# Sliding-window attention followed by a SiLU MLP: transposing q, k and the attention output by DMA over a DRAM scratch from the third batch on

## The chip, the cores and the metric

The kernel runs on one core of one Trainium2 chip. The metric is the device time of one execution in microseconds (us). The core has these engines: TensorE (PE; its weight loads are PEld), VectorE (DVE), ScalarE (ACT), GpSimd (POOL) and SyncE (SP). Besides them there are 16 DMA engines. In this kernel two of the engines issue DMAs: POOL, whose DMAs go through the software queue (q0), and SP, whose DMAs go through the hardware queue (q1).

Executions come in states: a run over 1.5% above the fastest of its kernel is called slow, and a single run has an unknown state.

## The reference, cut to what matters

```python
B, H, S, D = 8, 8, 576, 64          # batches, heads, tokens, head size
mask_plain = (rel >= 0) & (rel < 32)                        # heads 0..3
mask_dil   = (rel >= 0) & (rel < 128) & (rel % 4 == 0)      # heads 4..7
attn = softmax(where(mask, q @ k.T / 8, -1e9)) @ v
x = attn.transpose(0, 2, 1, 3).reshape(4608, 512)
h = x @ w_in                                                # 512 -> 2048
return (h * sigmoid(h)) @ w_out                             # 2048 -> 512
```

Inputs and outputs are float32. The kernel computes in float16. The MLP is by far the larger part of the arithmetic. Attention needs only a narrow band of scores, but in both kernels here it takes q and k with the head size on the partitions, and it hands its output to the MLP with the model size on the partitions. That is where the transposes come from.

## The kernel before

Each batch of attention loads q, k and v with converting DMAs from POOL (float32 in DRAM, float16 in SBUF). The token order is regrouped by `m, r` (token = 4m + r), so that a dilated head is a dense band in each residue r.

```python
def issue_qk(b):                       # four loads a batch, rows of 256 elements
    ...
        rows = src[b].rearrange("h (m r) d -> m h (r d)", r=DIL)
        for d, at in ((tiles[nm], m0), (rests[b % 2][p0 : p0 + MR], r0)):
            nc.gpsimd.dma_start(out=d.rearrange("p h r d -> p h (r d)"),
                                in_=rows[at : at + d.shape[0]])
def issue_v(b):                        # three loads a batch
    ...
    nc.gpsimd.dma_start(out=vp[:, j0:, :D], in_=win)      # rows of 64 elements
```

TensorE transposes q and k into PSUM, ACT and DVE evacuate them. After attention, TensorE transposes the output again, and a copy puts it in `xT`, in the regrouped token order:

```python
def trans_d(ring, h):
    for rp in range(2):
        for i, key in enumerate(("k", "rest", "q")):
            nc.tensor.transpose(tps[:, rp, i],
                loads[b][key][:, HN + h, 2 * rp : 2 * rp + 2, :], ident[:MA, :MA])
    yield "DVE", 0.40
    nc.vector.tensor_copy(...)
def x_d(ring, r):
    ...                                # 4 TensorE transposes
    dst = x_b[:, HP // 2 :, r * M : (r + 1) * M]          # contiguous
    ...                                # ACT copies it for batch 0, DVE for the others
    nc.vector.tensor_copy(dst, src)
```

The MLP works on groups of 512 tokens. A small planner in the Python code places attention steps between the four-matmul steps of the MLP and so fixes the order of the instructions on each engine. An output block leaves through `ob` (two buffers) with stores issued by SP.

The softmax here doesn't subtract the row's maximum and nothing guards it: scores larger than these inputs give would overflow.

## Time and profile before

| | before |
|---|---|
| median of 3 runs | 348.2 us (347.77 to 349.5) |
| PE busy | 325.1 us, 93% of the span |
| PE matmul instructions | 2656 |

The page of the profile comes first: the busy time of each engine, then rows with one digit for each of 40 equal slices of the span (9 is 90% busy or more), then the hardware DMA queue with packets, MB and the share of the 16 engines' time.

```profile
PE 325.1 (93%) x2656; PEld 165.1 (47%) x2656; DVE 221.7 (64%) x602; ACT 168.5 (48%) x322; POOL 53.1 (15%) x74
...
PE   0688898999989999999999999999999999999995
...
DMA  8999999929913972990589110100111200201232
...
q1 hardware_dynamic: 5632, 9.44, 9.1%
```

TensorE is the limit. DMA is full in the first 70 us or so (weights and the first batches of inputs), busy in bursts until about 190 us, and quiet after that. Next come the windows of 20 us. The columns are the busy time of PE, PEld, DVE, ACT and POOL (with instruction counts), the TensorE clock that the throttle granted as a share of full speed, the DMA share (1.00 is 16 engines' worth of packet time; overlapping packets count more than once) and GB/s.

```profile
120.00:140.00 20.00, 20.00 (x197) 10.71 (x198) 14.84 (x40) 11.21 (x23) 3.34 (x5) 1.00 0.59 69
200.00:220.00 20.00, 20.00 (x192) 10.02 (x190) 12.71 (x36) 11.95 (x25) 0.00 (x0) 1.00 0.10 28
```

From 120 us on TensorE is busy 20.00 of 20 us at full clock. Every microsecond of matmul taken away there should come off the time, unless it comes back as a wait.

This is one of the copies that put a transposed attention output in place. The view shows the engine, the duration in ns as minimum, median and maximum, when it ran, and the shape.

```profile
L421 DVE COPY xT<-xd_0_932 x1: 293/293/293, 65.0 to 65.0; 128x288 f16<-128x288 f16 x1
```

### The profile page before, as it was taken

The numbers are of one execution on the slowest core, as the hardware profiler recorded it, in microseconds if no ns is written. First come the engines' busy times: TensorE is split into PE (matmuls) and PEld (weight loads), VectorE is DVE, ScalarE is ACT, GpSimd is POOL, SyncE is SP. The second block draws the span as 40 slices with busy tenths as digits, with TensorE's granted clock in tenths as the row PEclk, the third lists the DMA queues.
The fourth block names the chain that finished last, engine by engine and source line by source line (L and its number), as shares of the span: only waits on it lengthen the run. The fifth ranks groups of instructions, "written<-read, shape, count | busy, mean of one in ns | idle before, by whom it ended". The sixth has DMA issues, their size and how long they took to land.

```text
span 348.7 us, 6693 instructions
## 1 busy us (share of the span) xinstructions
PE 325.1 (93%) x2656; PEld 165.1 (47%) x2656; DVE 221.7 (64%) x602; ACT 168.5 (48%) x322; POOL 53.1 (15%) x74
## 2 busy tenths in 40 slices
PE   0688898999989999999999999999999999999995
PEld 0553444555445455445554555455545444444442
DVE  4394777758888895888498739883986255054100
ACT  1453664076457546554644464546554254244211
POOL 8724344020203302030311000000000000000000
PEclk9999998999999999999999999999999999999999
DMA  8999999929913972990589110100111200201232
GB/s 107 188 205 199 200 181 169 189 53 141 109 30 37 178 55 59 132 120 32 89 127 103 31 36 27 32 32 30 32 31 32 60 11 22 77 14 32 61 82 70
DMA packets 59920, 29.80 MB, mean 85 GB/s; under 512 B 26608, under 2 KB 55280, under 8 KB 59888
## 3 DMA queue, kind: packets, MB, share of 16 engines
q0 software_dynamic: 54256, 19.92, 51.5%
q1 hardware_dynamic: 5632, 9.44, 9.1%
q8 instruction: 21, 0.34, 0.4%
q14 instruction: 11, 0.09, 0.1%
HBM read 39.84 MB, written 9.44 MB: 141 GB/s over the span
## 4 chain that ended last, share of the span: by engine, by line
PE 84%; DVE 9%; ACT 3%; DMA 2%; issue 1%; POOL 1%; ACTq 0%; POOLq 0%
DMA rest_111<-in_q_dram 2%; DVE gT_1066 L509 1%; PE y_1_892 L526 1%; PE y_3_3599 L526 1%; PE y_3_3089 L526 1%; PE y_3_2568 L526 1%; PE y_2_965 L526 1%; PE y_0_2117 L526 1%; PE y_0_664 L526 1%; PE y_3_4542 L526 1%; PE y_2_2464 L526 1%; PE y_2_2984 L526 1%; PE y_1_3338 L526 1%; PE y_1_3848 L526 1%; PE y_2_3495 L526 1%; PE y_3_1985 L526 1%
## 5 line engine op out<-in xcount | busy, mean ns | idle before, releaser
L498 PEld LDWEIGHTS <-w_in_83 128*128 128x128 f16 x576 | 52.8, 98 | 57.2 <-issue 6.1
L526 PEld LDWEIGHTS <-gT_4055 128*128 128x128 f16 x64 | 6.3, 98 | 7.5
L526 PEld LDWEIGHTS <-gT_3654 128*128 128x128 f16 x64 | 6.3, 98 | 7.6
L526 PEld LDWEIGHTS <-gT_4267 128*128 128x128 f16 x64 | 6.2, 97 | 7.6
L526 PEld LDWEIGHTS <-gT_3144 128*128 128x128 f16 x64 | 5.9, 98 | 6.4
L526 PEld LDWEIGHTS <-gT_519 128*128 128x128 f16 x64 | 5.8, 101 | 6.3 <-issue 1.4
L105 POOL DMA_DIRECT2D vraw_100<-in_v_dram x8 | 5.4, 678 | 20.7 <-DVE vd_98 L359 18.3
L105 POOL DMA_DIRECT2D vraw_101<-in_v_dram x8 | 5.4, 678 | 20.5 <-DVE vd_99 L359 14.7
L526 PEld LDWEIGHTS <-gT_1066 128*128 128x128 f16 x64 | 5.7, 98 | 5.8 <-DVE gT_1066 L509 0.4
L526 PEld LDWEIGHTS <-gT_2629 128*128 128x128 f16 x64 | 5.6, 97 | 5.1
L526 PEld LDWEIGHTS <-gT_2070 128*128 128x128 f16 x64 | 5.6, 97 | 5.1
L526 PEld LDWEIGHTS <-gT_1525 128*128 128x128 f16 x64 | 5.5, 97 | 4.9
L290 PE MATMUL td_0_205<-ident,k_nat_115 96*128 96x96 f16 x2 | 0.5, 272 | 6.6 <-DMA k_nat_115<-in_k_dram 6.6
L121 POOL DMA_DIRECT2D vp_97<-in_v_dram x4 | 5.7, 1432 | 1.5 <-DMA q_nat_167<-in_q_dram 1.4
L121 POOL DMA_DIRECT2D vp_96<-in_v_dram x4 | 5.8, 1444 | 0.6 <-PE td_3_678 L290 0.5
L290 PEld LDWEIGHTS <-rest_111 96*128 96x128 f16 x32 | 3.5, 108 | 5.1 <-issue 4.5
L311 PEld LDWEIGHTS <-kP_106 64*128 64x128 f16 x96 | 3.1, 100 | 5.7 <-issue 5.4
L273 ACT COPY kP_106<-ta_0_224 128x384 f16<-128x384 f16 x1 | 0.5, 479 | 10.9 <-PE ta_0_224 L270 10.9
L509 DVE SCALAR_TENSOR_TENSOR gT_4267<-th_0_4281,h_0_4268 128x512 f16<-128x512 f32 x1 | 0.7, 689 | 7.9 <-ACT th_0_4281 L507 7.9
L328 PEld LDWEIGHTS <-kqD_105 64*128 64x128 f16 x128 | 2.9, 97 | 5.8 <-issue 5.1
L365 PEld LDWEIGHTS <-probs_86 128*128 128x128 f16 x48 | 4.1, 100 | 3.1 <-DVE o_d_199 L368 0.8
L328 PEld LDWEIGHTS <-kqD_104 64*128 64x128 f16 x128 | 3.2, 102 | 5.2 <-issue 4.7
(1782 smaller groups left out, 1014.7 us busy)
## 6 DMA issues: line engine op xcount, KB each, us to landing
w_in_83<-in_moe_w_in_dram POOLq DMA_DIRECT2D x4, 512.0 KB, 12.1
w_out_84<-in_moe_w_out_dram POOLq DMA_DIRECT2D x4, 512.0 KB, 16.2
vp_97<-in_v_dram POOLq DMA_DIRECT2D x4, 384.0 KB, 10.8
vp_96<-in_v_dram POOLq DMA_DIRECT2D x3, 384.0 KB, 6.4
vraw_100<-in_v_dram POOLq DMA_DIRECT2D x4, 224.0 KB, 5.5
vraw_101<-in_v_dram POOLq DMA_DIRECT2D x4, 224.0 KB, 8.3
rest_111<-in_k_dram POOLq DMA_DIRECT2D x4, 192.0 KB, 6.2
rest_111<-in_q_dram POOLq DMA_DIRECT2D x4, 192.0 KB, 7.7
```

The lines of the kernel that those rows point to most:

```text
L105: nc.gpsimd.dma_start(out=vraw[p0 : p0 + m1 - m0, ab].rearrange("p h r d -> p h (r d)"), in_=src[m0:m1],)
L121: nc.gpsimd.dma_start(out=vp[:, j0:, :D], in_=win)
L273: nc.scalar.copy(kt[:, :MA], tps[:, 0].rearrange("p r m -> p m r"))
L290: nc.tensor.transpose(tps[:, rp, i], loads[b][key][:, HN + h, 2 * rp : 2 * rp + 2, :], ident[:MA, :MA],)
L311: nc.tensor.matmul(sp[i][:, QB * jj : QB * (jj + 1)], kP[r, hp, QB * j : QB * j + P], qP[r, hp, :, QM * j : QM * (j + 1)], start=True, sto ...
L328: nc.tensor.matmul(sp[i][:, c : c + MH], kqD[r, h, rp, 0, ab * KB : ab * KB + P], kqD[r, h, rp, 1, ab * MH : (ab + 1) * MH], start=True, s ...
L365: nc.tensor.matmul(a[:, i, : D + 1], lhs(i), rhs(i), start=True, stop=True)
L498: nc.tensor.matmul(h, w_in16[:, c, f * P : (f + 1) * P], xT[:, c, t0 : t0 + GT], start=(c == 0), stop=(c == HP - 1),)
L509: nc.vector.scalar_tensor_tensor(gTs[g][:, f], th, 1.0, h, ALU.add, ALU.mult)
L526: nc.tensor.matmul(y, gTs[g][:, f, tb * P : (tb + 1) * P], w_out16[:, f], start=(f == 0), stop=(f == NFF - 1),)
```

## The change

The intent is to take the transposes of q, k and the attention output off TensorE. Batches 0 and 1 keep the TensorE path. From batch 2 on, POOL issues a DMA that casts q and k into a float16 scratch in DRAM (a "cast"). SP then issues DMA transposes that read the scratch and write q and k transposed into SBUF (a "q/k turn": two instructions for heads 0 to 3 and two for heads 4 to 7). The attention output goes to another DRAM scratch, `x_s`, and comes back transposed, one group at a time (an "output turn"). Tokens keep their natural order, and the scores of a batch are made in 6 sets instead of 8.

```diff
-    xT = cpool.tile([P, HP, NT], F16, name="xT")
+    xA = cpool.tile([P, HP, GA * GT], F16, name="xA")                 # GA = 3
+    xRs = [cpool.tile([P, HP, GT], F16, name=f"xR_{i}") for i in range(XR)]  # XR = 3
+    kq_s = {b: dram.tile([2, H * S * D], F16, name=f"kq_s{b}") for b in range(PEB, B)}
+    x_s = dram.tile([NT, DM], F16, name="x_s")
...
+    def issue_cast(b):
+        for i, src in enumerate((k, q)):
+            nc.gpsimd.dma_start(
+                out=kq_s[b][i].rearrange("(p c) -> p c", c=2048),
+                in_=src[b].rearrange("h s d -> (h s d)").rearrange("(p c) -> p c", c=2048),
+            )
+    def issue_turn(b):
...
+            nc.sync.dma_start_transpose(out=dst[:, None, :], in_=win)      # 2 of these
...
+            nc.sync.dma_start_transpose(out=kqTs[b % 2][:, i], in_=rows)   # and 2 of these
...
+    def group_gen(g):
+        nc.sync.dma_start_transpose(out=x_of(g)[:, :, GT - n :], in_=x_s[t0 : t0 + n])
...
         def x_d(ring, r):
-            dst = x_b[:, HP // 2 :, r * M : (r + 1) * M]
+            dst = x_b[:, HP // 2 :].rearrange("p h (m r) -> p h m r", r=DIL)[:, :, :, r]
...
-                st.after = lambda: count(("T", b), H, lambda: issue_qk(b + 2))
+            if kind == "S" and b + 2 < B:            # after batch b's last scores
+                ... plan.push(turned[b + 2], turn_gen(b + 2), plan.t)
...
+                def loads():                         # after batch b's last use of v
+                    if b + 2 < B:
+                        issue_v(b + 2)
+                    if b + 3 < B:
+                        issue_cast(b + 3)
```

## The prediction

> **What bounds the kernel now.** TensorE. In the busy-time windows it is busy 20.0 of 20 us in each from 120 to 320 us, at full granted clock. In the timeline one four-matmul MLP step takes 0.863 us, so the 1152 MLP matmuls need about 248.5 us. The same step comes round every 35.57 us (third output block at 166.01, 201.57, 237.14 us): 27.6 us of MLP, about 8.0 us of one batch's attention. DVE (64%) and ACT (48%) have room. The page's DMA row reads 9 to full until about 60 us and is quiet after 200 us.
>
> **Removed.** Batches 2 to 7 lose 48 q/k transposes and 28 output transposes each. In the timeline the 96-column ones start 42.5 ns apart, the 72-column ones 33 ns: 48x42.5 + 12x43 + 16x33 ns = 3.1 us of TensorE a batch. Six instead of eight score sets compute the same blocks; each set costs TensorE a gap of about 0.1 us, so 0.2 us more. Six batches: about 19.7 us, all critical while PE is the limit. PSUM evacuations and pair copies leave ACT and DVE, worth nothing directly. Limit without new waits: about 328.5 us.
>
> **Added.** Per batch: a cast of q and k into DRAM (about as heavy as the old loads); transposes of 2x590 KB (overlapping windows) and 2x295 KB; 0.59 MB of output stored to DRAM, 0.5 MB per group transposed back. The trace has no DMA transpose. Its finest loads, 3072 rows of 256 B, land in 6.4 us, about 2 us of it fixed: some 23 ns per row per engine. As an estimate, 6912 rows of 256 B per q/k turn then take 10 us, 12 with the fixed part, and an output turn 5 us. [...]
>
> **Where it may come back.** The instruction order is fixed. In the new one, about 30 us of PE work lies between a q/k turn's issue and its use: safe. Between a batch's last attention matmul and its group's first MLP matmul lie 7.7, 10.3, 13.4, 18.6, 20 and 16 us of PE work; the chain (DVE, store to DRAM, landing, transpose) needs about 10 us, more if it queues behind the next q/k turn on the SP queue. I expect 2 to 6 us of waits at groups 2 and 3, none later, and a few us at batch 2's first scores, whose data come at the end of the crowded start (60 us or after). The head and the last 60 us stay.
>
> **Prediction: 333 us, 8 in 10 between 324 and 349.** Faster by over 2%: 0.70; within 2%: 0.18; slower: 0.12.
>
> **What would show it.** PE matmuls 2656 to 2200; a steady period of 32.3 instead of 35.6 us; hardware DMA queue up from 9.1% to 30 to 40%; q/k turn instructions landing in 4 to 12 us; PE waits for the transposed output of 2 to 6 us at groups 2 and 3, and for batch 2's k and q of 0 to 6 us. DVE loses about 25 us of busy time, ACT about 20, without effect.
>
> **What would make it wrong.** DMA transposes at half my rate: turns of 20 us or more, output turns queued behind them, about 10 us lost per group, which eats the gain. SP blocked inside transpose issues would hold back output stores, and with two output buffers ACT and then PE. The transposes could also slow the v loads on the same engines.

## The result

| | before | after |
|---|---|---|
| median, 4 runs each | 348.85 us (347.77 to 350.37) | 427.4 us (422.69 to 431.55) |
| ratio of fast runs | | 1.2142, 95% interval 1.2072 to 1.2212: slower |

A ratio here and below is the mean time of one kernel's fast runs over that of the other's of the same rounds, so it isn't quite the ratio of the medians. The two fast runs of the changed kernel took 425.13 and 422.69 us. Their mean, 423.9 us, is used below for differences. Its profile is of a run of 431.55 us, some 2% longer. The differences read from it below are of tens of us, and the same loss is in the fast runs.

The page of the changed kernel, same parts as before plus the row of the granted TensorE clock and the row of GB/s:

```profile
PE 307.7 (72%) x2200; PEld 148.1 (34%) x2200; DVE 200.6 (47%) x477; ACT 153.4 (36%) x258; POOL 43.1 (10%) x64
...
PE   0779980000079937990039986999999999999996
...
PEclk9999997555569986996559998999999999999999
DMA  9999999999999992999946995962312161010011
GB/s 124 194 197 204 195 89 61 48 64 65 98 187 216 211 160 75 124 68 41 179 100 65 181 194 142 161 168 78 90 36 76 50 128 49 24 75 24 26 73 73
...
q1 hardware_dynamic: 68720, 27.14, 43.8%
...
kq_s<-in_k_dram POOLq DMA_DIRECT2D x6, 576.0 KB, 21.8
```

The matmuls went as planned (2656 to 2200), but TensorE now stands still for two long stretches. In the first, DMA is at 9 in the DMA row while it moves only 48 to 98 GB/s; later it moves over 200. The DMA engines hold packets but hardly progress. The waits of TensorE, in total, times and longest, name what it stood still for:

```profile
PE s L402 <- DMA nat<-kq_s: 55.7, 1, 55.7
PE h L602 <- DMA xR<-x_s: 32.5, 2, 27.3
PE h L602 <- DMA xA<-x_s: 9.6, 1, 9.6
```

These three sum to 97.8 us. The predicted limit without new waits was 328.5 us, and 431.55 - 328.5 = 103.1 us, so they account for nearly all of it. One wait is for q and k of batch 2 (`nat` holds the turned heads 0 to 3), the others are for turned outputs: 9.6 us at group 2, 27.3 at group 3, and 5.2 at group 4.

Next is the timeline of the SP queue: start, duration, instruction, all in us. It shows how long SP took to get through each pair of DMA transposes.

```profile
50.32 56.30 SPq L130 DMA_TRANSPOSE nat<-kq_s  x2
106.66 14.57 SPq L134 DMA_TRANSPOSE kqT<-kq_s  x2
122.03 5.37 SPq L130 DMA_TRANSPOSE nat<-kq_s  x2
127.44 4.08 SPq L134 DMA_TRANSPOSE kqT<-kq_s  x2
...
137.34 13.22 SPq L130 DMA_TRANSPOSE nat<-kq_s  x2
...
174.48 34.92 SPq L130 DMA_TRANSPOSE nat<-kq_s  x2
209.45 2.73 SPq L134 DMA_TRANSPOSE kqT<-kq_s  x2
216.92 2.44 SPq L297 DMA_TRANSPOSE xR<-x_s  x1
```

The first q/k turn took SP 70.9 us, the second 9.5 us, for the same bytes. So the rate of a transpose is not simply low. The two worst are those at 50 and at 174 us; and the output turn at 216.92 stood behind the latter, which is the 27.3 us wait. The timeline of POOL shows what was issued near the two bad turns, and near the one at 137 us:

```profile
45.06 0.53 POOL L117 DMA_DIRECT2D kq_s<-in_k_dram  x1
...
59.80 1.44 POOL L154 DMA_DIRECT2D vp<-in_v_dram  x1 [1.02 <-PE av_p L438]
61.23 0.53 POOL L117 DMA_DIRECT2D kq_s<-in_k_dram  x1
...
136.15 0.53 POOL L117 DMA_DIRECT2D kq_s<-in_k_dram  x1
...
173.89 0.53 POOL L117 DMA_DIRECT2D kq_s<-in_k_dram  x1
```

Casts stand right beside the bad turns. But one stands beside the turn at 137 us too, which took 16.9 us with its second pair, so nearness alone is not enough. The packet records tell the two apart. At 137 us the fine v packets were through before the turn's packets began. The cast's 64 packets started at 139.69 us, mostly 13 to 15 were in flight at once, and they were over by 147.49; only 3 transpose packets started before 146 us. (The turn at 235 us was like that.) At 174 us the turn's packets were already running beside the v packets when the cast came. The 64 packets then lasted from 178.66 to 204.06 us, with about 12 in flight at first and then ever fewer, down to one. The windows, with the columns as before, show the stretches in which the core waits:

```profile
80.00:100.00 20.00, 0.00 (x0) 0.00 (x0) 0.00 (x0) 0.00 (x0) 0.00 (x0) 0.50 2.16 55
120.00:140.00 20.00, 18.81 (x167) 9.03 (x167) 14.25 (x35) 10.40 (x16) 3.86 (x5) 0.88 1.27 214
200.00:220.00 20.00, 0.00 (x0) 0.00 (x0) 0.00 (x0) 0.00 (x0) 0.00 (x0) 0.50 1.08 129
...
66.75:67.80 1.05, 0.00 (x0) 0.00 (x0) 0.00 (x0) 0.00 (x0) 0.00 (x0) 1.00 0.00 0
```

From 80 to 100 us no engine does anything and DMA moves 55 GB/s, against 214 GB/s between 120 and 140. The granted clock is 0.50 in that window. TensorE ran dry at 65.4 us and began again at 121.2; the granted clock was 0.50 from 70.1 to 124.7 us and 1.00 after that. It is a small extra price of this long wait: from 120 to 140 us, where TensorE was busy again, the mean was 0.88. The last line of the windows is the most telling. It is a window of 1.05 us in the middle of the first bad turn, in which not one packet starts on any of the 16 DMA engines. Here are the packet records around it: start, duration and end in us, queue, bytes; some records left out. Packets of 18432 bytes are the casts; those of 256 bytes on q1 are the transposes; those of 128 and 512 bytes on q0 belong to the v loads.

```
  start     duration      end     queue bytes
  66.487    + 1.376      67.863   q0    18432
  66.663    + 0.031      66.694   q0    128
  66.665    + 0.031      66.696   q0    128
  66.675    + 1.378      68.053   q1    256
  66.685    + 1.375      68.060   q0    128
  66.690    + 5.759      72.449   q0    18432
  66.694    + 1.373      68.067   q0    128
  66.706    + 1.374      68.080   q1    256
  66.745    + 1.340      68.085   q1    256
  (nothing starts for 1.10 us)
  67.845    + 0.031      67.876   q1    256
```

The packets of 128 bytes at 66.663 and 66.665 took 31 ns. Those that started 20 to 80 ns later took 1.34 to 1.38 us, and so did the transposes' packets of 256 bytes: just the 1.376 us of one cast packet. The second cast packet shown was itself held up, to 5.759 us. In that window 8 cast packets are in flight, six of them from before the listing. One is enough, though: from 102.00 to 106.17 us a single cast packet is in flight at a time (102.00 to 103.38, 103.41 to 104.78, 104.79 to 106.17 us). During each, 30 to 82 other packets start, and then none for 0.84 to 1.11 us, nearly until it ends. Statistics of packet durations over the bad turn, and after it, in ns:

| packet | 50 to 120 us: median, mean, longest | 120 to 135 us: median, mean |
|---|---|---|
| 256 bytes (transposes) | 31, 177, 5835 | 18, 22 |
| 128 bytes (v) | 32, 109, 2813 | |
| 18432 bytes (cast) | 1376, 1775, 8308 | |

The theory that follows from this (A): while DMA transposes are in flight, the 16 DMA engines move in step, and one long packet on one engine holds up all of them, fine v loads included. Where the casts' long packets come at different moments on different engines, the whole machine would by this theory pay for them one after the other. The sizes allow it: as an estimate, the 133 cast packets that the trace has from 50 to 120 us, of 1.376 us each, would take 11.4 us if all 16 engines worked through them independently, and up to 183 us if one after the other. The first rival (B) is that transposes are slow beside any load, the fine v loads above all. The second (C) is that there are too many bytes for the DMA engines in that stretch. The third (E) is that casts into DRAM are harmful as such. The last (D), which none of the first expectations names, is that there is nothing odd in the DMA engines and the order in which SP issues its work is the cause.

### The profile page after: what moved, and what is told of

Its sections match the earlier page's. It is cut to its first block, busy times and chain, and to the rows that moved or that the text cites. A ratio compares the mean times of both kernels' runs of the same rounds, so it can differ in the third digit from the quotient of the medians.

```text
span 429.8 us, 5645 instructions
## 1 busy us (share of the span) xinstructions
PE 307.7 (72%) x2200; PEld 148.1 (34%) x2200; DVE 200.6 (47%) x477; ACT 153.4 (36%) x258; POOL 43.1 (10%) x64
## 2 busy tenths in 40 slices
DMA packets 109370, 47.41 MB, mean 110 GB/s; under 512 B 82592, under 2 KB 104352, under 8 KB 108960
## 3 DMA queue, kind: packets, MB, share of 16 engines
q1 hardware_dynamic: 68720, 27.14, 43.8%
## 4 chain that ended last, share of the span: by engine, by line
PE 62%; another core or an unknown queue 13%; DMA 8%; DVE 7%; SPq 5%; ACT 2%; issue 1%; POOL 1%; ACTq 0%; POOLq 0%
PE h L602 28%; PE y L630 27%; SPq L130 4%; DMA x_s<-oD 3%; PE s L402 2%; DMA xR<-x_s 2%; DMA nat<-in_q_dram 2%; DVE gT L613 2%; PE av_d L438 2%; DVE oD L442 2%; PE av_p L438 1%; DVE oP L442 1%; DVE probs L417 1%; ACT th L611 1%
## 5 line engine op out<-in xcount | busy, mean ns | idle before, releaser
L613 DVE SCALAR_TENSOR_TENSOR gT<-th,h 128x512 f16<-128x512 f32 x144 | 98.0, 683 | 95.9 <-ACT th L611 95.8
L630 PE MATMUL y<-w_out,gT 128*128 128x512 f16 x576 | 141.1, 384 | 0.9 <-DVE gT L613 0.4
L611 ACT ACTIVATE th<-h 128x512 f32<-128x512 f32 x144 | 86.1, 598 | 128.8 <-PE h L602 122.3
L602 PE MATMUL h<-xR,w_in 128*128 128x512 f16 x384 | 95.1, 388 | 32.5 <-DMA xR<-x_s 32.5
L602 PEld LDWEIGHTS <-w_in 128*128 128x128 f16 x576 | 54.6, 100 | 106.9 <-issue 52.9
L630 PEld LDWEIGHTS <-gT 128*128 128x128 f16 x576 | 54.1, 99 | 61.3 <-issue 2.7
L410 ACT ACTIVATE probs<-s 128x768 f16<-128x768 f32 (+2 forms) x45 | 36.4, 809 | 72.7 <-PE s L402 72.7
L602 PE MATMUL h<-xA,w_in 128*128 128x512 f16 x192 | 50.7, 397 | 11.6 <-DMA xA<-x_s 9.6
L402 PE MATMUL s<-nat 64*128 64x96 f16 x144 | 6.7, 217 | 55.7 <-DMA nat<-kq_s 55.7
L438 PEld LDWEIGHTS <-probs 128*128 128x128 f16 x448 | 23.7, 102 | 15.8 <-issue 2.4
L442 DVE TENSOR_TENSOR oD<-av_d,rcps 72x256 f16<-72x256 f32 x64 | 26.9, 420 | 2.2
L154 POOL DMA_DIRECT2D vp<-in_v_dram x8 | 11.5, 1442 | 75.8 <-PE av_p L438 71.6
```

Source lines behind the costliest of these rows:

```text
L402: nc.tensor.matmul(sp[i][:, w * n : w * (n + 1)], lhs, rhs, start=True, stop=True)
L410: nc.scalar.activation(p2, both[:, :, :n], AF.Exp, scale=scale)
L438: nc.tensor.matmul(a[:, i, : D + 1], lhs(i), rhs(i), start=True, stop=True)
L442: nc.vector.tensor_tensor(o, a[:n, :, :D], rcp[:n, :, None].broadcast_to([n, HN, D]), ALU.mult)
L602: nc.tensor.matmul(h, w_in16[:, c, f * P : (f + 1) * P], x_g[:, c], start=(c == 0), stop=(c == HP - 1),)
L611: nc.scalar.activation(th, h, AF.Tanh, scale=0.5)
```

## The experiments

Unless a median of several runs is given, a kernel got one run, of unknown state; single runs are used only where the differences are tens of us or the question is whether a wait is there at all. The runs came in three groups, each with its own runs of the kernel before on the same chip: 348.64 us for e1 to e4, 349.68 us for e6 to e9, 350.01 us for e10 to e12 (medians of 7 runs each).

### e1_one_cast: take the casts away

Only batch 2 is cast; every turn reads its scratch. Batches 3 to 7 get wrong q and k (the check of the result doesn't notice it, so its "correct" says little about q and k in any run here).

```diff
+    kq_one = dram.tile([2, H * S * D], F16, name="kq_s")
+    kq_s = {b: kq_one for b in range(PEB, B)}
     def issue_cast(b):
+        if b > PEB:
+            return
```

> The kernel after with the cast of batch 2 alone; all later turns (the DMA transposes of q and k) read batch 2's scratch, so batches 3 to 7 are wrong on purpose. v loads and everything else stay. Theory A (a cast in flight beside a transpose, with its 18432-byte packets, makes both crawl): no turn over 15 us of SP issue time, PE waits for turned k and q under 10 us, 330 to 345 us. Theory B (the fine v loads collide with the transposes): still 410 us or more. Theory C (just too many bytes for the DMA engines in the middle stretch): part of it back, 370 to 400 us.

Measured: 344.89 us. All the turns and all the v loads are still there. The waits of TensorE and one window:

```profile
PE s L405 <- DMA nat<-kq_s: 4.9, 1, 4.9
...
PE h L605 <- DMA xR<-x_s: 3.5, 1, 3.5
```

```profile
80.00:100.00 20.00, 18.57 (x159) 8.87 (x158) 17.44 (x45) 10.91 (x19) 2.13 (x2) 1.00 1.35 221
```

The same window now moves 221 GB/s instead of 55. Packets of 256 bytes took 31 ns on average from 50 to 120 us, instead of 177. About 79 us (423.9 - 344.9) are gone with the five casts. Rival B falls: transposes beside v loads alone do not freeze, though they aren't undisturbed either (9.8 to 21 us of SP a turn, where theory A had at most 15).

### e2_tiny_v: keep the casts, take most of the v loads away

```diff
         src = v[b, HN:].rearrange("h (m r) d -> m h (r d)", r=DIL)
+        if b >= PEB:
+            for ab in range(2):
+                nc.gpsimd.dma_start(out=vraw[:16, ab]...[:, :1], in_=src[:16, :1])
+            nc.gpsimd.dma_start(out=vp[:16, HN * NB - 1, :D], in_=v[b, 0, :16])
+            return
```

> The kernel after with all casts kept, and the v loads of batches 2 to 7 cut to three tiny ones that wait for the same readers (results wrong on purpose). Theory A (casts collide): 405 to 430 us, the first turn still takes tens of us. Theory B (fine v loads collide): 335 to 350 us. Theory C (bytes): 370 to 400 us.

Measured: 345.88 us (the result is wrong). The expectation of theory A as it then stood missed: the casts are all there, and there is no freeze. Rival B's range was hit, but B had fallen in e1: the v loads are needed for the freeze, and do not make it alone.

```profile
80.00:100.00 20.00, 18.56 (x151) 8.70 (x149) 15.77 (x38) 10.78 (x19) 1.97 (x4) 1.00 1.10 200
```

From 50 to 120 us the trace has 211 cast packets here and 133 in the changed kernel, so the long packets are not fewer. The difference is when they come. In the packet records between 60 and 70 us 16 cast packets are in flight at once, and all 64 of a batch are over in 6.6 us. In the changed kernel there are 26 stretches of over 0.5 us between 50 and 121 us in which no packet starts; 1 to 8 cast packets are in flight in them, 3.3 on average, and the casts go on until 120.8 us. Both queues got about equal numbers of packets through there: from 65 to 70 us the changed kernel's trace has 133 packet starts of q0 and 132 of q1. The author's guess, which no run shows by itself, is that a cast that lies in q0 among thousands of fine v packets is reached by different engines at different times. Theory A was mended: the freeze needs long packets that are out of step across the engines, and a transpose in flight. The two cases in the changed kernel itself, at 137 and at 174 us, speak for it. One thing in this trace does not fit it well: for some 5.6 us between 50 and 121 us, 1 to 8 cast packets were in flight here too, with transposes, and yet packets went on starting (never a break over 0.12 us). So what the v loads add may be more than to put the casts out of step; that stays open.

### e3_small_cast: shorter packets

The casts' rows are cut from 2048 to 512 elements.

```diff
-                out=kq_s[b][i].rearrange("(p c) -> p c", c=2048),
+                out=kq_s[b][i].rearrange("(a p c) -> p a c", a=4, c=512),
```

> The kernel after with each cast cut into rows of 512 elements, so that a packet writes 1024 instead of 18432 bytes; same bytes, same moments, correct results. Theory A with packet length as the cause (an engine busy with a 1.38 us packet holds up a transpose that needs all engines): the crawl is mostly gone, 335 to 365 us. Theory A with any DRAM-to-DRAM cast as the cause, whatever its packets: 410 to 430 us. Theory B or C: 410 to 430 us.

Measured: 396.44 us median (393.45 to 400.72), ratio 1.1322 (1.1248 to 1.1397). That is a miss for the size: some 28 us of the loss go (fast runs, 423.9 to 395.4), not 60 or more. The packets became 1024 bytes of 98 ns on average, and the mean of the 256-byte packets fell to 44 ns (22 where nothing disturbs). The first turn took 34.4 us instead of 70.9, and no stretch of over 0.13 us without a packet start is left between 50 and 121 us. So the standstills go with the long packets. The waits of TensorE show where most of the rest is:

```profile
PE h L602 <- DMA xR<-x_s: 24.4, 2, 18.8
PE s L402 <- DMA nat<-kq_s: 15.8, 1, 15.8
```

The wait for q and k fell from 55.7 to 15.8 us. What is left is mostly waits for turned outputs (24.4 and 9.1 us) and for output buffers (11.0 us), behind turns of 12 to 34 us on SP. Why the turns still take so long was not settled. One reading is that each of the 3513 cast packets between 50 and 120 us now holds the others up a little; no run shows this apart.

### e4_one_scratch: casts and turns never at the same time

With one scratch for all batches, the dependencies let a cast start only when the turn before has read the scratch, and a turn only when its cast has landed.

```diff
-    kq_s = {b: dram.tile([2, H * S * D], F16, name=f"kq_s{b}") for b in range(PEB, B)}
+    kq_one = dram.tile([2, H * S * D], F16, name="kq_s")
+    kq_s = {b: kq_one for b in range(PEB, B)}
```

> The kernel after with one scratch for q and k instead of six, so that each cast has to wait until the turn before it has read the scratch, and the turn for its cast: casts and turns never overlap. Correct results, same bytes. Theory A: 335 to 355 us, no turn issue over 15 us. Theory B: 410 us or more (v loads still overlap turns). Theory C (bytes): 410 us or more, as the same bytes have less room.

Measured: 381.57 us median (379.07 to 382.26), ratio 1.0909 (1.0842 to 1.0975). Another miss, and an instructive one. The freeze is gone: no pair of turn instructions takes longer than 13.20 us. Rival C falls with it, since the page has the same 47.41 MB as that of the changed kernel. But the waits of TensorE moved to the output:

```profile
PE h L603 <- DMA xA<-x_s: 21.1, 1, 21.1
PE h L603 <- DMA xR<-x_s: 16.8, 2, 12.3
PE y L631 <- ACT ob L642: 9.7, 3, 8.8
```

The timeline of SP shows why:

```profile
98.12 13.20 SPq L131 DMA_TRANSPOSE nat<-kq_s  x2
111.42 3.56 SPq L135 DMA_TRANSPOSE kqT<-kq_s  x2
115.08 1.92 SPq L476 DMA_DIRECT2D x_s<-oD  x2
119.60 5.19 SPq L298 DMA_TRANSPOSE xA<-x_s  x1
```

SP took its work in program order. A q/k turn that is needed much later (batch 4's, from 98.12 us) stands ahead of the store of batch 2's output (115.08) and of that group's output turn (119.60). SP holds still first for the cast and then for about 17 us of turn. So rival D is a real second cost here, where SP also has to wait for the casts. In e1, which keeps the changed kernel's order on SP without casts to wait for, TensorE waited only 5.8 us for turned outputs; so the order alone does not make the large loss.

### e9_plain_copy: is it the conversion?

This is e1 with the missing casts replaced by plain float32 copies from DRAM to DRAM, in the same places, which nobody reads.

```diff
     def issue_cast(b):
+        if b > PEB:
+            for i, src in enumerate((k, q)):
+                nc.gpsimd.dma_start(out=junk[b][i].rearrange("(p c) -> p c", c=2048),
+                                    in_=src[b]....rearrange("(p c) -> p c", c=2048))
+            return
```

> The run with one cast (e1, 345 us), with a plain DRAM-to-DRAM copy of q and k, float32 without conversion, put where each missing cast stood: packets of 36864 bytes that should take an engine as long (about 1.4 us). Batches 3 to 7 still read batch 2's scratch. If a long packet on one engine freezes all engines while transposes are in flight, whatever it does: the crawl is back, 400 to 440 us, first turn over 30 us. If the conversion is what hurts: about 345 us.

Measured: 443.26 us. The freeze is back:

```profile
PE s L411 <- DMA nat<-kq_s: 60.3, 1, 60.3
```

```profile
80.00:100.00 20.00, 0.00 (x0) 0.10 (x1) 0.00 (x0) 0.00 (x0) 0.00 (x0) 0.50 1.89 102
```

The long packets (36864 bytes here, median 1364 ns) do it; the conversion isn't needed. (All long packets tried went from DRAM to DRAM; none into SBUF was tried beside a transpose.) Nor is any dependency on the scratch, since nobody waits for these copies. Against e1, only traffic was added.

### e12_cast_no_turn: the control without transposes

All q, k and outputs are transposed on TensorE (the kernel of e8 below), and the six casts are issued in their old places beside the v loads; nobody reads them. The edit is shown against e8; the first cast and the scratch are put back with it.

```diff
-                    if PEQ <= b + 3 < B:
+                    if b + 3 < B:
                         issue_cast(b + 3)
```

> Control for the freeze: e8 (no DMA transpose anywhere, 353.5 us) with the six casts of the change added beside its loads, at the same moments as in the change; nothing reads them. If a long packet freezes all engines only while transposes are in flight: 352 to 358 us, and fine packets still start on other engines while a cast packet runs. If casts beside fine loads are slow by themselves: 380 us or more.

Measured: 352.82 us, against 353.45 us for the same kernel without casts (in another group of runs, whose kernel before took 349.68 instead of 350.01 us).

```profile
80.00:100.00 20.00, 17.20 (x181) 9.42 (x180) 18.34 (x51) 9.18 (x16) 3.80 (x5) 1.00 1.49 206
```

Here 198 cast packets ran from 50 to 120 us with a mean of 1378 ns and a longest of 1508, and the v packets of 128 bytes beside them had a mean of 35 ns and a longest of 141. Its expectation also asked whether fine packets still start while a cast packet runs. They do: in the time with 1 to 8 cast packets in flight, 292 other packets start per us and the longest break is 0.37 us, against 131 per us and breaks up to 1.15 us in the changed kernel. Rival E falls: casts beside fine loads, in the same queue, cost this kernel nothing, as long as no transpose is in flight. With e1, e2, e9 and e12 three things are each needed for the freeze: long packets, the fine v loads, and transposes.

### e7_pe_qk: only the output over DMA

To see the parts of the change apart, the limit `PEB` was split in two: q and k on TensorE for batches below `PEQ`, the output on TensorE below `PEX`. This one has natural order, 6 score sets, no casts, no q/k turns.

```diff
+    PEQ = 8
+    PEX = 2
```

> The other half: q and k of all batches transposed on TensorE from the loads of the kernel before, only the attention output goes over DRAM. No casts, no turns of q and k, so nothing with long packets beside a transpose. TensorE loses 28 transposes a batch, about 1.04 us, six times, and two score sets: 341 us with no waits; the order leaves 7 to 12 us for the output chain, which may cost a few us at group 2: 338 to 348 us. If any DMA transpose beside the fine loads stalls: over 355 us.

Measured: 337.82 us median (337.29 to 337.89), ratio 0.9656 (0.9631 to 0.9681): faster. There is no wait for a turned output at all. The output half of the change is a gain, as predicted, and a little larger than this run's expectation, which had 341 us without waits; why was not taken apart.

### e8_pe_all: only natural order and 6 score sets

```diff
+    PEQ = 8
+    PEX = 8
```

> Only the natural token order and six score sets, no DMA transpose at all. Same TensorE work as before but for two score sets of 0.1 us gap each in eight batches: 345 to 350 us.

Measured: 353.45 us median (353.02 to 353.5), ratio 1.0105 (1.0083 to 1.0126), so 1% longer instead of the small gain that was expected. The group of output copies on DVE (busy us, mean ns, then idle before):

```profile
L511 DVE COPY xA<-xd 128x288 f16<-128x288 f16 x28 | 21.4, 798 | 1.0 <-PE h L617 0.8
```

The same copy took 293 ns before, into a contiguous destination. In natural order its destination has a step of four tokens, and it takes 2.7 times as long; no run here shows why it is this much. DVE's busy time rose to 234.7 us. That this is the cause of the few us is argued from these numbers and from small new waits of TensorE on DVE; the copies alone were not put back.

### e6_pe_out: only q and k over DMA

One scratch as in e4, outputs on TensorE.

```diff
+    PEQ = 2
+    PEX = 8
+    kq_one = dram.tile(...)            # as in e4
```

> q and k turned by DMA over one scratch (so that casts and turns never overlap, as in e4), but the attention output of all batches transposed on TensorE and copied by DVE, as in the kernel before. No output chain can queue behind a turn. If e4's remaining 37 us of waits for the transposed output are that queueing: about 336 us (328.5 and 1.04 us of output transposes for each of six batches, and a few us of waits), 333 to 345. If the waits of e4 come from elsewhere: 360 us or more.

Measured: 355.13 us median (354.96 to 356.16), ratio 1.0162 (1.0137 to 1.0187). Missed by more than 10 us. TensorE waited 10.3 us (once 9.1) for output buffers:

```profile
PE y L646 <- ACT ob L657: 10.3, 5, 9.1
```

The stores of finished output blocks stood behind a turn on SP. TensorE also waited 4.0 us on DVE, which carries the slow copies of e8. The rest was not taken apart. With this order of SP the gain from q and k isn't collected.

### e10_turn_last: mend the order

From batch 4 on a q/k turn is issued after the output turn of batch b-2 and the next cast after it, with one scratch and three output buffers. Then neither a cast nor an output chain can meet the turn. The v loads, which POOL issues after the cast, come behind the turn too, and the third buffer was not tried alone; so several things change at once.

```diff
     # in stored(b), after the output turns of batch b were issued:
+            if PEQ <= b + 2 < B:
+                plan.push(turned[b + 2], turn_gen(b + 2), plan.now)
     # in turn_gen(b):
+        if b - 2 >= PEX and b + 1 < B:
+            issue_cast(b + 1)
...
-            ob = o32.tile([P, DM], F32, tag="ob", bufs=2, ...)
+            ob = o32.tile([P, DM], F32, tag="ob", bufs=3, ...)
```

> Meant to keep the whole change and take both costs away: one scratch (casts and turns cannot overlap), from batch 4 on each q/k turn is issued after the output chain of the batch before it in the queue instead of ahead of it, its next cast right after it, and a third output buffer. Correct results. If the freeze and the queueing behind the turn are all that the change loses: about 330 us, 326 to 338, under e7 (337.8). If moving the turn late makes the scores wait for it: 340 to 360 us with PE waits for the turned k and q.

Measured: 343.41 us median (342.63 to 344.17), ratio 0.9824 (0.9794 to 0.9854): unclear, on the edge of the 2%. It misses the range. One long wait is left, for the first turned output:

```profile
PE h L622 <- DMA xA<-x_s: 14.7, 1, 14.7
```

The turns of batches 2 and 3 are still issued by the old rule, in the crowded start. Batch 3's turn (73.91 to 89.38 us on SP) stands ahead of batch 2's output stores, which issue only at 90.57, and the output turn comes at 107.30. But the last stretch isn't order: for 11.5 us SP waited for the stores to land. In the packet records the stores' 512-byte packets start only 0 to 18 times per us from 93 to 100 us, in turn with the long packets of the cast issued at 91.12, and then share the engines with v packets until 106. No transpose is in flight there. So here a long packet also held up a short transfer in the other queue that someone waits for.

### e11_turn_from4: and leave the start alone

As e10, but q and k go over DMA only from batch 4 on; outputs from batch 2 on as before.

```diff
-    PEQ = 2
+    PEQ = 4
```

> As e10, but q and k go over DRAM from batch 4 on, so that no turn falls into the crowded first 90 us. TensorE keeps 48 transposes of 42.5 ns in two more batches than e10, 4.1 us. If e10 suffers at the start: 332 to 338 us and below e10; if it does not: 4 us above e10.

Measured: 330.96 us median (329.01 to 331.54), ratio 0.9451 (0.9415 to 0.9488): faster, and better than both kernels. TensorE waited for only one turned output, and for no q/k turn:

```profile
PE h L622 <- DMA xR<-x_s: 0.9, 1, 0.9
```

The timeline of SP shows the new order, output turn first:

```profile
98.62 1.51 SPq L303 DMA_TRANSPOSE xA<-x_s  x1
100.31 5.36 SPq L133 DMA_TRANSPOSE nat<-kq_s  x2
105.71 3.61 SPq L137 DMA_TRANSPOSE kqT<-kq_s  x2
```

This q/k turn occupied SP for 5.36 + 3.61 = 9.0 us; the three later ones took 7.5 to 8.7 us.

## Why the prediction was wrong

The verdict (faster) and the time (333 us, 8 in 10 between 324 and 349) were wrong: it was 427.4 us, and 423.9 in the fast runs. The step that failed is the cost of the cast, which stands fourth below. Point by point:

- **What bounds the kernel: right.** Where the new waits are absent, matmul work taken off TensorE comes off the time (e7: 349.68 to 337.82 us; e11: 350.01 to 330.96 us).
- **What is removed: right in size.** The prediction had 456 fewer matmul instructions, which came out exactly. It took 19.7 us off with q and k of six batches moved. e11 moves those of four, so 2 x 48 x 42.5 ns = 4.1 us stay, and 15.6 us were to be had; e11 gained 19.1 us on the kernel before of its group (350.01 to 330.96 us). The third output buffer came with it, and what the rest of the surplus is was not taken apart. In the changed kernel DVE lost 21 us of busy time instead of 25, ACT 15 instead of 20. The slower output copies of the first batches were overlooked: the four of batch 1 took DVE 790 ns each, which is 2 of the missing 4 us.
- **"6912 rows of 256 B per q/k turn then take 10 us": right for an undisturbed turn,** even a little high (7.5 to 9.0 us on SP in e11). Beside v loads alone it was too low for most turns (9.8 to 21 us in e1). The prediction took its rate from the fine loads of the kernel before, as that trace has no DMA transpose. The fixed part of about 2 us is of the size that this trace shows: a v load of 160 KB issued at 84.81 us landed 3.2 us later, 1.4 us of it before its first packet and some 0.3 us after its last. The windows of e11 that hold these turns moved 199 to 227 GB/s, mixed with other traffic.
- **"A cast of q and k into DRAM (about as heavy as the old loads)": this is the step that failed.** It counted bytes. A cast is cheap by bytes (e12), but its packets of 18432 bytes last 1.38 us, and beside a turn and the fine v loads they stopped the start of all other packets for up to 1.15 us at a time. The first turn took 70.9 us of SP's time, where the prediction had 12 us to landing. Taking the casts away (e1) is worth some 79 us.
- **"About 30 us of PE work lies between a q/k turn's issue and its use: safe": wrong as a consequence** and, at the start, in itself. For batch 2 the turn was issued at 50.3 us and TensorE ran dry at 65.4. The prediction had allowed 0 to 6 us there; e1 has 4.9 without the freeze, the changed kernel 55.7.
- **"I expect 2 to 6 us of waits at groups 2 and 3": the mechanism was right, the size wrong.** They were 9.6 and 27.3 us, and 5.2 us came at group 4, where none was expected. The second is the output turn behind a q/k turn of 37.7 us on SP. The prediction named such queueing among what would make it wrong, but thought of transposes at half the rate.
- **"The transposes could also slow the v loads": right,** and they slowed each other: 128-byte packets had a mean of 109 ns, against 34 ns in e1.
- **The DMA queue: outside the range.** q1's share was 43.8% against the predicted 30 to 40%; a share counts held-up packets as busy (2.16 of DMA share at 55 GB/s from 80 to 100 us). In e11, with fewer turns and no freeze, it was 29.8%.
- **Steady period of 32.3 us: not testable.** The changed kernel never reached a steady state.

What is shown: the freeze needs transposes (e12), long packets (e1, e3, e9) and the fine v loads (e2); the order on SP is a second cost (e4), and e11, which changes the order, the overlaps and the start together, has neither. What is argued: that to put the casts out of step is what the v loads do (the packet records show casts in flight at once with e2, and in the changed kernel itself at 137 us, and spread where it froze; but no run put the casts out of step by other means, and e2 has moments that do not fit). e1, e2, e9 and e12 are single runs of unknown state; e9 against e1 and e12 is a difference of some 90 us or more. Open: why the DMA engines stood still together at all.

## What to carry to other kernels

As far as this kernel shows: cost a DMA that runs beside a DMA transpose by the length of its packets (1.38 us each here, and some 79 us for five casts) and by what shares its queue, not by its bytes alone. Keep long packets and transposes apart in time, by a dependency if need be (in e4 no pair of turn instructions took over 13.20 us, against 56.30), and keep them away from a short store that a chain waits for (11.5 us in e10). Then look at the issuing queue as at an engine in program order: put the transfer that is needed first ahead of the prefetch, and start such prefetches only when the crowded start is over (343.41 us in e10, 330.96 in e11). When DMA is "busy" at a quarter of its usual GB/s (55 against 214 here), look at single packets: a window without a single packet start (1.05 us here) says more than any average.
